# A state-space scan and an ELU layer on one core: the words of the next pair's scan result made on two engines, second-layer steps laid between its last products, and weight words of one group made a step sooner

## The chip, the cores and the metric

The program runs on one core of a Trainium2 chip. The number that counts is the device time of one execution in microseconds (us). The core has a matrix engine (PE, with a separate track PEld for its weight loads), a vector engine (DVE), a scalar engine (ACT), a general engine (POOL), a queue that only issues transfers (SP), and 16 DMA engines. Each engine takes its own instructions in order; between engines, semaphores order the work.

## The reference

The first block is a Mamba-2 scan over 4 batches, 8 heads, 768 positions (head size 32, state size 16), in chunks; the second is a dense layer pair of 256 to 2048 to 256 with an ELU between:

```python
y_intra = np.einsum('bhij,bhjd->bhid', CB * L, xc)                 # inside a chunk
y_inter = np.einsum('bhin,bhnd->bhid', Cc, state) * exp(cum)       # from the state before it
y[:, :, sl] = y_intra + y_inter
...
x = y.transpose(0, 2, 1, 3).reshape(3072, 256)
h = x @ w_in                                                       # first layer, 256 -> 2048
g = np.where(h > 0, h, np.exp(np.minimum(h, 0)) - 1)
out = g @ w_out                                                    # second layer, 2048 -> 256
```

The two weight matrices come as 64-bit floats and are put together as 32-bit floats in the kernel.

## The kernel before, in words

The 3072 tokens are cut into 12 blocks of 256. Blocks 0 to 3 go through the first layer one at a time in plain 32-bit products (`l1`, L666). Blocks 4 to 11 go in pairs (n = 4, 6, 8, 10), 512 tokens at a time, and their first layer is made of "words": both operands are split into a high word and a rest that PE can multiply in its faster `fp32r` form. Three pairs of products per 128 columns (`l1_words`, L770 to L794) write two PSUM tiles, `ps_h` (high words and low words) and `ps_w` (a product of sums, `y_both` with `w_words`). ACT copies `ps_w` to `e` (L787), DVE adds it into `ps_h` (L790), ACT makes the two parts of the ELU in `begin_end` (L796, L797) and DVE ends it in `end_words` (L804), which is called inside the next `l1_words`.

The words of the scan's result come from `words_of_y` (L749) and `both_of_y` (L763): for each of the two halves k of the 256 features, `y1` is y times a constant (L756), `y0` is a difference (L758), and `y_both` a sum (L768). All six are DVE instructions on 128 x 512 elements. The words of `w_in` come from `words_of_w` (L731), once for each of the eight 256-column pieces: an ACT multiplication (L736) and a DVE one (L737).

The second layer of a pair is `second` (L863), a generator. It works by Strassen-Winograd: two halves of seven "quarters", each quarter four `yield`s, 56 steps in all. A step is two 32-bit products of 128 x 128 x 128 (L898), each done by PE in two passes, so four PE records and four weight loads. After a quarter's fourth step its sums are taken out of PSUM by `add` on DVE (L876) or a copy on ACT. Quarters use in turn one of the seven buffers of the pool `ps_a`, which everything else shares, and the single buffer of the pool `ps_o`. The quarter r = 5 of the second half and the quarter r = 0 of the next pair's `second` both use that single buffer.

The order of the work is written out by hand. While pair n is in its first layer (k = 0 to 15), `l2s(count)` lays so many steps of the second layer of pair n-2 behind each `l1_words(n, k)`, and the scan of the next pair m = n+2 is laid in between. At k = 9 come the scan's scores, sums and states; at k = 13 `across` (L594, products of C with the chunk's starting state, PSUM tiles `ps_y`, L613) and then `inside` (L622, products inside the chunk, L632). `inside` adds to the same four PSUM tiles and takes them to `yT` by six ACT instructions (L651). With k = 15 the pair is done; 48 of the 56 steps have been laid by then. Then `words_of_y(m)` and `both_of_y(m)` follow, `end_words()` for k = 15, and the eight steps that are left: the quarters r = 5 and r = 6 of the second half. The next instruction of PE is the first product of `l1_words(m, 0)`, behind its six products come the first steps of the next `second`, quarter r = 0. This passage, from k = 13 of one pair to k = 0 of the next, is called a pair boundary here; there are three (m = 6, 8, 10). For m = 4, `words_of_y(4)` and `both_of_y(4)` are called from the loop over the plain blocks (L1222 and L1224).

In that loop (n = 2, 3, eight steps i each), `scan_ahead(2, i)` (L1139) also makes the words of `w_in`, piece by piece, by the list of L1156; the output of a plain block leaves through one ACT copy (`ob`, L829) from the single `ps_o` buffer.

Of the kernel before, what the change touches and what calls it, by code (L numbers as in the profile page):

```python
# [14 lines left out]
ALU = mybir.AluOpType  # L15
ACT = mybir.ActivationFunctionType
# [5 lines left out]
WORD = 2.0 ** 12  # L22
NEAR = 1.0 + 2.0 ** -13
# [8 lines left out]
def kernel(  # L32
# [27 lines left out]
    nc = tc.nc  # L60
# [21 lines left out]
    def psum(shape, name):  # L82
        return p_a.tile(shape, F32, tag="a", name=name)
# [7 lines left out]
    for k in range(4):  # L91
        (nc.scalar if k % 2 else nc.sync).dma_start(
            out=la0[BH * k:BH * (k + 1)],
# [182 lines left out]
    for v in range(2):  # L276
        nc.gpsimd.affine_select(
            out=low16[Q * v:Q * v + Q], in_=low16[Q * v:Q * v + Q], pattern=[[1, Q]],
# [5 lines left out]
        out=hmask, in_=hmask, pattern=[[-N, NH]], compare_op=ALU.is_ge, fill=0.0,  # L284
        base=0, channel_multiplier=1)
    nc.gpsimd.affine_select(
        out=hmask, in_=hmask, pattern=[[N, NH]], compare_op=ALU.is_ge, fill=0.0,
# [8 lines left out]
        out=minus, in0=ident, scalar1=-1.0, scalar2=None, op0=ALU.mult)  # L296
# [213 lines left out]
    def decay(n, q):  # L510

        decay_of(n, 2 * q)
        decay_of(n, 2 * q + 1)
# [82 lines left out]
    def shift(n, v):  # L596


        return 2 * D * v if n else 0
# [21 lines left out]
    def inside(y, *ns):  # L621


        for t in range(2):
            for at, n in enumerate(ns):
                s = st[n]
                for u in range(2):
                    for v in range(2):
                        toks = slice(Q * v, Q * v + Q)
                        for q in range(4):  # L630
                            h, col = 4 * t + q, (D * q + shift(n, v)) % P
                            nc.tensor.matmul(  # L632
                                out=y[t][v][col:col + D, at, u],
                                lhsT=s["x"][toks, u, D * h:D * (h + 1)],
                                rhs=s["M"][h // 2][toks, u, h % 2], start=False, stop=True,
                                tile_position=(Q * v, col), skip_group_check=True)
            n = ns[0]
            if n // 2 not in yT:
                yT[n // 2] = ffn.tile([P, KC, 2, 2, P], F32, tag="yT", name="yT")
            out = yT[n // 2][:, t, n % 2:n % 2 + len(ns)]  # L640
            for v in range(2):
                k = shift(n, v)
                for at in (0, k) if k else (0,):
                    count, src = P - k, (at + k) % P
                    to, src = out[at:at + count, :, :, Q * v:Q * v + Q], y[t][v][src:src + count]
                    if t and n == 1:
                        nc.vector.tensor_copy(to, src)
                    elif n < 4:
                        nc.scalar.copy(out=to, in_=src)
                    else:  # L650
                        nc.scalar.activation(to, src, ACT.Copy, scale=WORD)  # L651
        for n in ns:
            st.pop(n)
# [96 lines left out]
    def words_of_y(n):  # L750

        y = yT[n // 2].rearrange("p k b u i -> p k (b u i)")
        y1 = conv.tile([P, KC, 2 * BLK], F32R, tag="y1", name="y1", bufs=1)
        y0 = conv.tile([P, KC, 2 * BLK], F32R, tag="y0", name="y0", bufs=1)
        for k in range(KC):
            nc.vector.tensor_scalar(  # L756
                out=y1[:, k], in0=y[:, k], scalar1=NEAR / WORD, scalar2=None, op0=ALU.mult)
            nc.vector.scalar_tensor_tensor(  # L758
                out=y0[:, k], in0=y1[:, k].bitcast(F32), scalar=WORD, in1=y[:, k],
                op0=ALU.mult, op1=ALU.subtract)  # L760
        y_words[n] = y1, y0
# [11 lines left out]
    def l1_words(n, m):  # L773

        cols = slice(m % 2 * P, (m % 2 + 1) * P)
        w, w0 = k_words[m // 2]
        w1, both_w, w0 = w[:, 0, :, cols], w[:, 1, :, cols], w0[:, :, cols]
        y1, y0, both_y = y_words[n]
        high, both = psum([P, 2 * BLK], "ps_h"), psum([P, 2 * BLK], "ps_w")
        passes = [(high, w1, y1), (high, w0, y0), (both, both_w, both_y)]  # L780
        for ps, lhs, rhs in passes if m == 0 else passes[2:] + passes[:2]:
            for k in range(KC):
                nc.tensor.matmul(  # L783
                    out=ps, lhsT=lhs[:, k], rhs=rhs[:, k], start=k == 0 and lhs is not w0,
                    stop=k == KC - 1 and lhs is not w1)
        e = ffn.tile([P, 2 * BLK], F32, tag="e", name="e", bufs=2)
        nc.scalar.copy(out=e, in_=both)  # L787
        if late:
            end_words()
        nc.vector.scalar_tensor_tensor(  # L790
            out=high, in0=high, scalar=1.0 - 1.0 / WORD, in1=e, op0=ALU.mult, op1=ALU.add)
        late.append((n, m, high, e))
# [209 lines left out]
    y = across(0)  # L1002
# [132 lines left out]
    def weigh_two(m, q):  # L1135
        weigh(m, q)
        weigh(m + 1, q)

    def scan_ahead(n, i):  # L1139


        m = 4
        if n == 2:
            if i < 2:
                load_b(m + i)
                load_bc(m + i)
                spread_exp(m + i)
            if i == 2:
                spread_cum(5)
                load_x(m)  # L1150
                load_x(m + 1)
            if i > 1:
                decay(m + i // 6, (i - 2) % 4)
            if i > 2:
                turn_part(m + i // 6, i % 3)
            for p in ((), (), (), (), (0,), (1, 2), (3, 4), (5, 6))[i]:  # L1156
                words_of_w(p)
            if i in (5, 6):
                low_of_w(i - 5)
            return  # L1160
        if i == 0:
            turn_part(5, 2)
            scaled(m, nc.gpsimd)
            scaled(m + 1, nc.gpsimd)
        if i < 2:
            decay(m + 1, i + 2)
        if i == 0:
            words_of_w(7)
        if i == 2:
            turn_part(4, 3)  # L1170
            turn_part(5, 3)
            scores(m, m + 1)
            sums(m, m + 1)
            for q in range(4):
                weigh(m, q)
                weigh(m + 1, q)
            states(m)
            states(m + 1)
        if i in (0, 1):
            load_bc(i + 6)  # L1180
        if i == 2:
            for to in (6, 7):
                load_b(to)
                spread_cum(to)
        if i == 1:
            low_of_w(2)
        if i > 5:
            turn_part(6, i - 6)

    def turn_step(n, k, late):  # L1190
        m = n + 2
        if m == NP or k > 7:
            return
        if m == 6:
            steps = [(6, 2), (7, 0), None, (7, 1), None, (7, 2), (6, 3), (7, 3)]
            if steps[k // 2 * 2 + late]:
                turn_part(*steps[k // 2 * 2 + late])
        else:
            at = k // 2 * 2 + late
            turn_part(*[(m, 0), (m, 1), (m, 2), (m + 1, 0), (m + 1, 1), (m + 1, 2), (m, 3), (m + 1, 3)][at])  # L1200
# [75 lines left out]
    for n in range(4, NP, 2):  # L1276
        m = n + 2 if n + 2 < NP else None
        steps = second(n - 2)

        def l2s(count):  # L1280
            for _ in range(count):
                next(steps)

        for k in range(16):
            l1_words(n, k)
            turn_step(n, k // 2 * 2 + 1, k % 2)
            if n == 4 and k % 2 and k < 8:
                next(left)()
            if n == 4 and k in (1, 3, 5, 8, 10):
                low_of_w({1: 3, 3: 4, 5: 5, 8: 6, 10: 7}[k])  # L1290
            if n == 4 and k == 2:
                sum_t1(2, 7)
            if m:
                stage_scan(n, k)
            begin_end()
            if k == 0 and n > 4:
                store(n - 4, 0)
                store(n - 4, 1)
            if not m:
                l2s(4 if k % 2 else 3)  # L1300
                continue
            l2s((3, 3, 3, 3, 3, 3, 3, 3, 4, 4, 2, 2, 3, 3, 3, 0)[k])
            if k == 9:
                scores(m, m + 1)
                sums(m, m + 1)
                for q in range(4):
                    weigh_two(m, q)
                states(m)
                l2s(3)
            if k == 10:  # L1310
                states(m + 1)
            if k == 13:
                inside(across(m, m + 1), m, m + 1)
        if m:
            words_of_y(m)
            both_of_y(m)
        end_words()
        for _ in steps:
            pass
# [35 lines left out]
```

## Time and profile before

| what | value |
|---|---|
| runs of the kernel before | 354.31 us (353.54 to 355.02, 3 runs) |
| the profiled execution | 354.31 us, of which the span of its instructions is 352.4 us |
| around the span | 1.9 us |
| PE busy | 341.7 us, 97% of the span |
| DVE, ACT, POOL busy | 257.6, 230.1, 199.3 us (73%, 65%, 57%) |
| granted PE clock | full in all 40 slices |
| PE instruction queue q8 | 31 packets, 0.51 MB in all |

How to read it: a busy share is an average over stages, and PE matmuls are pipelined, so a record's duration is longer than what the next record has to wait. What one matmul costs is the distance between the starts of two in a row: 112 ns for a pass of L898, 231 ns for a product of L783, some 7 to 15 ns for a product of L613 or L632. A line such as `[0.33 <-DVE c_sum L876]` gives the idle time of the engine before the instruction and what ended it; "issue" stands where the engine waited for nothing that the profile shows.

### The profile page before, as it was taken

The numbers are of one execution on the slowest core, as the hardware profiler recorded it, in microseconds if no ns is written. First come the engines' busy times: TensorE is split into PE (matmuls) and PEld (weight loads), VectorE is DVE, ScalarE is ACT, GpSimd is POOL, SyncE is SP. The second block draws the span as 40 slices with busy tenths as digits, with TensorE's granted clock in tenths as the row PEclk, the third lists the DMA queues.
The fourth block names the chain that finished last, engine by engine and source line by source line (L and its number), as shares of the span: only waits on it lengthen the run. The fifth ranks groups of instructions, "written<-read, shape, count | busy, mean of one in ns | idle before, by whom it ended". The sixth has DMA issues, their size and how long they took to land.

```text
span 352.4 us, 9890 instructions
## 1 busy us (share of the span) xinstructions
PE 341.7 (97%) x3894; PEld 300.8 (85%) x3894; DVE 257.6 (73%) x532; ACT 230.1 (65%) x527; POOL 199.3 (57%) x309
## 2 busy tenths in 40 slices
PE   8889999999999999999999999999999999999996
PEld 5668888887888889798898988899988899999996
DVE  4898979896999868875878775877775856666232
ACT  4789989799525798566599557599557366555000
POOL 5554554563740299985196764196854173455860
PEclk9999999999999999999999999999999999999999
DMA  8969998561152510160331170230000100000002
GB/s 147 235 201 193 299 187 228 112 103 50 46 87 62 125 47 11 19 149 4 91 74 32 12 155 4 74 63 2 3 1 4 60 1 2 1 2 31 31 1 62
DMA packets 72727, 26.50 MB, mean 75 GB/s; under 512 B 57768, under 2 KB 67560, under 8 KB 72680
## 3 DMA queue, kind: packets, MB, share of 16 engines
q1 hardware_dynamic: 70360, 25.60, 31.1%
q8 instruction: 31, 0.51, 0.7%
q10 hardware_dynamic: 2320, 0.26, 0.5%
q14 instruction: 16, 0.13, 0.1%
HBM read 22.51 MB, written 3.34 MB: 73 GB/s over the span
## 4 chain that ended last, share of the span: by engine, by line
PE 67%; DVE 9%; ACT 9%; POOL 7%; issue 3%; SPq 2%; DMA 2%; POOLq 0%; DVEq 0%; ACTq 0%
PE ps_o L898 26%; PE ps_h L666 12%; PE ps_h L783 11%; PE ps_w L783 6%; PE ps_o L823 6%; DVE ps_h L790 2%; POOL g L839 2%; PE ps_y L632 2%; POOL w L839 2%; DMA w<-in_moe_w_in_dram 2%; POOL L L523 2%; DVE g L804 1%; PE ps_g L538 1%; ACT yT L651 1%; DVE y L758 1%
## 5 line engine op out<-in xcount | busy, mean ns | idle before, releaser
L898 PEld LDWEIGHTS ps_o<-w_out,g 128*128 128x128 f32 x640 | 78.4, 191 | 5.9 <-DVE c_sum L876 2.2
L898 PE MATMUL ps_o<-w_out,g 128*128 128x128 f32 x640 | 80.7, 276 | 1.2 <-DVE c_sum L876 1.1
L804 DVE SCALAR_TENSOR_TENSOR g<-e,ps_h 128x512 f32<-128x512 f32 x64 | 43.9, 686 | 33.3 <-ACT e L797 32.9
L796 ACT ACTIVATE e<-ps_h 128x512 f32<-128x512 f32 x64 | 38.2, 597 | 43.5 <-DVE ps_h L790 43.4
L839 POOL TENSOR_TENSOR g<-g 128x256 f32<-128x256 f32 x32 | 23.3, 730 | 72.8 <-DVE g L804 65.4
L666 PE MATMUL ps_h<-yT,w_in 128*128 128x256 f32 (+1 forms) x272 | 60.4, 371 | 2.0 <-POOL w_in L245 1.9
L666 PEld LDWEIGHTS ps_h<-yT,w_in 128*128 128x128 f32 x272 | 48.4, 190 | 9.6 <-POOL w_in L245 3.1
L790 DVE SCALAR_TENSOR_TENSOR ps_h<-ps_h,e 128x512 f32<-128x512 f32 x64 | 44.6, 697 | 10.4 <-ACT e L787 7.5
L787 ACT COPY e<-ps_w 128x512 f32<-128x512 f32 x64 | 36.8, 575 | 19.3 <-PE ps_w L783 19.3
L783 PE MATMUL ps_w<-y_both,w_words 128*128 128x512 f32 x128 | 45.1, 433 | 0.0
L518 ACT ACTIVATE L<-L,ncum 128x64 f32<-128x64 f32 x160 | 42.5, 337 | 0.2
L797 ACT ACTIVATE e<-e 128x512 f32<-128x512 f32 x64 | 40.4, 632 | 2.0
L783 PE MATMUL ps_h<-y,w_words 128*128 128x512 f32 x128 | 40.5, 397 | 0.0
L783 PE MATMUL ps_h<-y,w 128*128 128x512 f32 x128 | 39.7, 391 | 0.0
L898 PE MATMUL ps_o<-w_sum,g 128*128 128x128 f32 x304 | 38.3, 275 | 0.0
L898 PEld LDWEIGHTS ps_o<-w_sum,g 128*128 128x128 f32 x304 | 37.1, 192 | 1.1
L523 POOL TENSOR_SCALAR_AFFINE_SELECT L<-L 64x512 f32<-64x512 f32 x40 | 29.1, 728 | 10.3 <-ACT L L518 8.2
L823 PE MATMUL ps_o<-w_out,g 128*128 128x256 f32 x128 | 30.7, 382 | 0.7 <-ACT ob L829 0.7
L839 POOL TENSOR_TENSOR g<-t,g 128x256 f32<-128x256 f32 x40 | 28.1, 736 | 5.7 <-PE ps_o L898 5.7
L839 POOL TENSOR_TENSOR t<-g 128x256 f32<-128x256 f32 x40 | 28.8, 752 | 2.4 <-DVE g L852 2.1
L783 PEld LDWEIGHTS ps_h<-y,w 128*128 128x128 f32 x128 | 24.0, 188 | 5.6
L839 POOL TENSOR_TENSOR g<-g,t 128x256 f32<-128x256 f32 x40 | 28.1, 736 | 0.2
(130 smaller groups left out, 531.3 us busy)
## 6 DMA issues: line engine op xcount, KB each, us to landing
L<-flat SPq DMA_DIRECT2D x20, 256.0 KB
w<-in_moe_w_out_dram SPq DMA_DIRECT2D x8, 512.0 KB
w<-in_moe_w_in_dram SPq DMA_DIRECT2D x7, 512.0 KB
xr<-in_x_dram SPq DMA_DIRECT2D x24, 128.0 KB
out_dram<-c_sum SPq DMA_DIRECT2D x9, 256.0 KB
bc<-in_B_dram SPq DMA_DIRECT2D x24, 64.0 KB
bc<-in_C_dram SPq DMA_DIRECT2D x22, 64.0 KB
ec<-flat_exp SPq DMA_DIRECT2D x10, 128.0 KB
```

The lines of the kernel that those rows point to most:

```text
L518: nc.scalar.activation(L[:, h, u], L[:, h, u], ACT.Exp, bias=ncum[:, u, row:row + 1])
L523: nc.gpsimd.affine_select(out=part, in_=part, pattern=[[0, 4], [0, 2], [1, Q]], compare_op=ALU.is_ge, fill=0.0, base=0, channel_multiplier=-1)
L666: nc.tensor.matmul(out=ps[:, j, toks], lhsT=w_in[i][:, k, j * P:(j + 1) * P], rhs=yT[n // 2][:, k, n % 2].rearrange("p u i -> p (u i)")[:, ...
L783: nc.tensor.matmul(out=ps, lhsT=lhs[:, k], rhs=rhs[:, k], start=k == 0 and lhs is not w0, stop=k == KC - 1 and lhs is not w1)
L787: nc.scalar.copy(out=e, in_=both)
L790: nc.vector.scalar_tensor_tensor(out=high, in0=high, scalar=1.0 - 1.0 / WORD, in1=e, op0=ALU.mult, op1=ALU.add)
L796: nc.scalar.activation(e, high, ACT.Relu, scale=-1.0)
L797: nc.scalar.activation(e, e, ACT.Exp, scale=-1.0)
L804: nc.vector.scalar_tensor_tensor(out=g_of[n, m].rearrange("p b i -> p (b i)"), in0=e, scalar=1.0, in1=h, op0=ALU.subtract, op1=ALU.max)
L823: nc.tensor.matmul(out=o_of[n][:, ts], lhsT=g_of[n, j][:, m % 2, ts * P:(ts + 1) * P], rhs=w_out[:, m], start=(m == 0 and ts == 0), stop=( ...
L839: nc.gpsimd.tensor_tensor(out=out, in0=in0, in1=in1, op=ALU.subtract)
L898: nc.tensor.matmul(out=ps[:, ts], lhsT=b[:, ts * P:(ts + 1) * P], rhs=a[:, i], start=(i == chunk[0] and ts == 0), stop=(i == chunk[-1]), s ...
```

## The change

Three edits.

In `words_of_y` the two multiplications that make `y1` are taken out of the loop: the half k = 1 goes to ACT, the half k = 0 stays on DVE, and both stand ahead of the two differences `y0`.

```diff
+        nc.scalar.activation(y1[:, 1], y[:, 1], ACT.Copy, scale=NEAR / WORD)
+        nc.vector.tensor_scalar(
+            out=y1[:, 0], in0=y[:, 0], scalar1=NEAR / WORD, scalar2=None, op0=ALU.mult)
         for k in range(KC):
-            nc.vector.tensor_scalar(
-                out=y1[:, k], in0=y[:, k], scalar1=NEAR / WORD, scalar2=None, op0=ALU.mult)
             nc.vector.scalar_tensor_tensor(
                 out=y0[:, k], in0=y1[:, k].bitcast(F32), scalar=WORD, in1=y[:, k],
                 op0=ALU.mult, op1=ALU.subtract)
```

In the loop over pairs, `words_of_y(m)` moves from behind the loop to k = 15, between `l1_words` and `begin_end`. Four of the eight last steps (the quarter r = 5 with its DVE sum) are laid ahead of `both_of_y(m)` and `end_words()`. At k = 13, one of the three steps stays ahead of `across`, and two go between `across` and `inside`.

```diff
         for k in range(16):
             l1_words(n, k)
+            if m and k == 15:
+                words_of_y(m)
...
-            l2s((3, 3, 3, 3, 3, 3, 3, 3, 4, 4, 2, 2, 3, 3, 3, 0)[k])
+            l2s((3, 3, 3, 3, 3, 3, 3, 3, 4, 4, 2, 2, 3, 1, 3, 0)[k])
...
             if k == 13:
-                inside(across(m, m + 1), m, m + 1)
+                y = across(m, m + 1)
+                l2s(2)
+                inside(y, m, m + 1)
         if m:
-            words_of_y(m)
+            l2s(4)
             both_of_y(m)
         end_words()
```

In `scan_ahead` the pieces of `w_in` whose words are made at i = 3 to 6 shift: piece 0 from i = 4 to i = 3, piece 1 from i = 5 to i = 4, piece 3 from i = 6 to i = 5; pieces 2, 4, 5 and 6 keep their place.

```diff
-            for p in ((), (), (), (), (0,), (1, 2), (3, 4), (5, 6))[i]:
+            for p in ((), (), (), (0,), (1,), (2, 3), (4,), (5, 6))[i]:
                 words_of_w(p)
```

## The prediction

> **What bounds the kernel now.** The page comes first.
>
> ```profile
> PE 341.7 (97%) x3894; PEld 300.8 (85%) x3894; DVE 257.6 (73%) x532; ACT 230.1 (65%) x527; POOL 199.3 (57%) x309
> ...
> q8 instruction: 31, 0.51, 0.7%
> ```
>
> PE is busy 97% of the span and the change takes no product from it, so only PE's waits can be won. The second line is kept for later: PE's instructions come in by 31 transfers of 16 KB, and 3894 + 3894 records over 31 is 251, so about 256 instructions a transfer. Next is the list of waits of PE, of which three rows lie in what the change touches (total us, times, longest).
>
> ```profile
> PE ps_y L632 <- issue: 1.9, 3, 0.7
> PE ps_o L898 <- DVE c_sum L876: 1.1, 3, 0.4
> PE ps_o L823 <- ACT ob L829: 0.7, 1, 0.7
> ```
>
> Two come once at each of the three pair boundaries, the third once at a plain block's end. These idle times count from modelled ends; I price from starts. The timeline of the first boundary (m = 6) shows both:
>
> ```profile
> 160.51 1.17 ACT L651 ACTIVATE yT<-ps_y 128x256 f32<-128x256 f32 x3
> ...
> 161.48 0.69 PE L632 MATMUL ps_y<-M,xr 64*32 64x64 f32 x45 [0.74 <-issue]
> ...
> 162.14 1.18 ACT L651 ACTIVATE yT<-ps_y 128x256 f32<-128x256 f32 x3 [0.46 <-PE ps_y L632]
> ...
> 166.60 0.69 DVE L790 SCALAR_TENSOR_TENSOR ps_h<-ps_h,e 128x512 f32<-128x512 f32 x1
> ...
> 167.20 0.57 DVE L756 TENSOR_SCALAR y<-yT 128x512 fp32r<-128x512 f32 x1
> 167.32 0.60 ACT L796 ACTIVATE e<-ps_h 128x512 f32<-128x512 f32 x1 [0.89 <-DVE ps_h L790]
> 167.80 0.69 DVE L758 SCALAR_TENSOR_TENSOR y<-y,yT 128x512 fp32r<-128x512 f32 x1
> ...
> 168.41 0.42 DVE L756 TENSOR_SCALAR y<-yT 128x512 fp32r<-128x512 f32 x1
> 168.87 0.69 DVE L758 SCALAR_TENSOR_TENSOR y<-y,yT 128x512 fp32r<-128x512 f32 x1
> 169.48 1.29 DVE L768 SCALAR_TENSOR_TENSOR y_both<-y,yT 128x512 fp32r<-128x512 f32 x2
> ...
> 170.80 0.62 PE L783 MATMUL ps_w<-y_both,w_words 128*128 128x512 f32 x2
> 171.28 0.75 DVE L876 TENSOR_TENSOR c_sum<-ps_o,c_sum 128x256 f32<-128x256 f32 x2
> ...
> 171.75 1.61 PE L898 MATMUL ps_o<-w_out,g 128*128 128x128 f32 x12 [0.33 <-DVE c_sum L876]
> ```
>
> PE arrives at 171.75 with the first step of the next `second`, whose PSUM tile is the single `ps_o` buffer. Quarter r = 5 was finished by PE near 168.3, but its sum (the first L876 at 171.28) stands in DVE's queue behind six word instructions and `end_words`.
>
> **The sum ahead of `y_both`, words on two engines.** PE's two last products start at 170.80 and 171.03 and each lasts 0.23 before the next can start, so unhindered r = 0 starts at 171.27 instead of 171.75: 0.48 lost. The same three lines at m = 8 read 224.13 and 225.27 (free at 224.59: 0.68 lost), at m = 10 277.46 and 278.38 (277.92: 0.46). Together 1.62 us.
>
> Does the new order free the buffer in time? DVE's starts in a row (the pace, shorter than the durations) are 0.60 for the first L756, 0.61 for L758 and L768, 0.46 for the second L756, and 0.34 for L876 (165.13 to 165.47 in this timeline). New queue at m = 6: L790 166.60, y1 167.20, y0 167.80, y0 168.41, sum of r = 5 169.02, `y_both` 169.36 and 169.97, `end_words` 170.58, sum of r = 6 171.19. The buffer is free at 169.43 (169.02 + 0.41), 1.8 before PE needs it. One L756 (0.46) leaves DVE and one L876 (0.34) steps ahead, so the last `y_both` ends near 170.65, 0.1 earlier than before, and PE needs it at 171.03. At m = 8 the margin is thinnest: 224.17 against 224.36. PE's next waits of this kind hold: the whole 1.62 is gained unless something else moves.
>
> The ACT half costs nothing here. ACT ends its copy (L787) at 166.44, then idles 0.89 until L790 ends. The same form, an ACT multiplication into `fp32r` of 128 x 512, takes 613 ns (L736): 166.46 to 167.07, before 167.32. The new wait is DVE's second y0 on it, at 168.41, late by more than 1 us. Queued behind it on ACT are only the two ELU parts of k = 15, for which `end_words` waits at 170.58. If the cover went, the cost would be 0.2 to 0.6 a boundary. At m = 4 the ACT half follows six `yT` copies that end at 111.87, so it pushes the next ELU (L679 at 112.15) by about 0.3; DVE has one instruction less there, and the first `y_both` product has 0.77 to spare. Zero.
>
> The row against the rule: L736 takes 613 ns on ACT, L756 421 ns on DVE. The Trainium skill, "ScalarE: Activation LUTs", section "Rules for kernel authors", says to put a multiplication on VectorE and not on ScalarE. By it this half should lose 0.19 us at each of four places, 0.8 in all, if ACT were what PE waits for; the row with 0.89 idle says zero.
>
> **Steps between `across` and `inside`.** What would they fill? The gap at 161.48 falls in the middle of `inside`, before an instruction with no semaphore to wait for. From start to start (160.52 to 161.48, 213.97 to 214.69, 267.24 to 268.06) it takes 0.95, 0.72 and 0.82, 2.5 us in all. I read it as PE waiting for its instructions. First: the three gaps stand 1281 and 1279 PE instructions apart in program order, five blocks of 256. Second: queue q8 has one transfer just before each gap, landing at 160.12, 213.30 and 266.69; PE goes on 1.36, 1.39 and 1.37 later. Third: the next transfer starts 1.12, 1.17 and 1.14 after each gap's end, as if a block's first instruction asks for the block after next. So a transfer is asked for about 1.14 before it starts (157.6, 211.2, 264.3), and PE may run only 256 instructions until it is there, 3.5 to 3.8 us later. `across` and `inside` issue 64 and 128 passes, each with a weight load, at 7 to 15 ns: the block is used up in 2.8 us.
>
> The point that decides: at 157.6, 211.2 and 264.3 PE has already begun the three steps of k = 13 (they start at 157.5, 210.9, 264.2). The moved steps lie inside the window in both orders. The same 256 instructions stand between request and gap, only in another sequence. So two steps (0.9 us) later in the row take 0.9 us away from the front, PE runs dry at the same instruction and the same time, and the gap stays. Bounds from the rows: below, nothing is filled (0); above, 0.90 a boundary fills nearly all of 0.95 and the whole of 0.72 and 0.82. I take 0, nearest to the count of instructions, and keep the other end as a rival.
>
> Row against rule once more: transfers land and PE still waits 1.4 us. The Trainium skill, "Runtime: NRT & Kernel Launch", section "Instruction fetch mechanics", agrees on 16 KiB blocks of 256 instructions but says that prefetch is hidden because dispatch is slower than the fill. By that rule the gap is no fetch, and the steps could fill it: 351.0; by the rows 352.6.
>
> What else moves: `across` starts two steps earlier. Its starting states left POOL at 156.3 at the latest, and it would start near 158.0. The sums of r = 3 end some 0.2 later on DVE, before the ELU end it does next at 160.51. Nothing on SP moves.
>
> **A group of `w_in` words sooner.** PE waits at 83.20 for ACT's `ob` copy: 83.20 instead of 82.38, 0.82 lost. Before the copy ACT runs the two L736 of i = 6; one moves to i = 5, one each from 5 to 4 and 4 to 3. That shortens the queue only where ACT rests between:
>
> ```profile
> 66.00:82.60 16.60, 16.38 (x43) 1.00 0.46 88
> ```
>
> ACT is busy 16.38 of these 16.60 us. The same instructions stand ahead of `ob`, so it ends at the same time, less one rest of 0.09 before L679 at 70.79. Bounds: a loss where the shifted words delay a `w_out` piece (0.52 spare at 74.04, and the 0.82 wait that follows swallows it), a gain up to one L736, 0.52. I take 0.09.
>
> **Sum.** 1.62 + 0 + 0.09 = 1.7 us, from 354.31 (span 352.4 plus 1.9 around it; this execution is also the median of the runs shown) to **352.6**. PE is the limit after each boundary, and the spare time of its other waits there is 0.4 or more, or set by PE itself, so I carry the gain whole.
>
> **Rivals.**
>
> *The gap is filled too.* For: two steps take 0.90 us, about a gap. Against: the count of instructions. Then the chain of `yT` copies sets r = 0: the copies' own wait goes (0.46 at m = 6, none at m = 8 where six run on end, 0.33 at m = 10), the last `y_both` ends at 170.2, 224.2, 276.9, and r = 0 starts 1.26, 0.82 and 1.18 earlier. With 0.09: 354.31 - 3.35 = 351.0.
>
> *The gain is given back.* ACT is busy 20.75 of the 22.5 us after the boundary (171.5 to 194), and the chain of copy, L790, L796, L797 does not start sooner, since it waits for the same last word product. If PE, 0.5 ahead, runs into a PSUM buffer that ACT or DVE has not freed, the gain ends there: 354.2. Against: no such wait there has less than 1 us to spare.
>
> *Slower: `across` meets a buffer that ACT still holds.* Before, its fourth tile takes the buffer that the `ps_w` copy of k = 13 frees; at m = 8 this ends at 212.42, just as PE comes. If, 0.9 earlier, a tile still needs that copy, PE's sequencer stands before the point at which the next block is asked for: later by 0.7 (158.34 for 157.64), 1.2 (212.42 for 211.20) and 0.9 (265.19 for 264.28), 2.8 in all: 354.31 - 1.7 + 2.8 = 355.4. It decides as soon as the buffer comes free later than those requests. Against: in the new order r = 4's step asks for a buffer after the four tiles and not before, so one that is free longer is left for them.
>
> **Numbers.** Forecast 0.52, filled gap 0.22, gain given back 0.16, slower 0.10. A run of this kernel can tell about 0.5% from no change (1.8 us; 352.54 is the border). The forecast lies on it: half of its chance is faster. Faster: 0.26 + 0.22 = 0.48. Slower by over 0.5% needs the slow rival together with the gain given back: 0.05. Same: 0.47. The range reaches from 350.6 (filled gap, 0.4 less for the spread of runs) to 354.6 (gain given back, the same spread), and leaves out the slow rival and tails.
>
> **What would show it.** Right: at k = 0 of each new pair L898 follows L783 after 0.23, with no wait for L876; one ACT multiplication stands between L787 and L796 in ACT's idle time; the "issue" gap in L632 remains with 0.7 to 0.95, on 1280 instructions' distance; L823 still waits near 83 for `ob`. Wrong: the gap is gone or lies elsewhere, or a wait for ACT in `across`, or L783 waiting for `y_both`.

## The result and the profile after

The changed kernel takes 352.48 us (median of 6 runs, 352.12 to 352.69); the kernel before, on the same chip, 355.12 us (6 runs, 353.54 to 355.68). The ratio is 0.9932 with a 95% interval of 0.9911 to 0.9953. The profiled execution takes 352.12 us, its span is 350.3 us. From L755 on, line numbers are one higher than before: L784 is the product of `l1_words`, L899 that of `second`, L877 the sum.

The page's engine row:

```profile
PE 341.5 (98%) x3894; PEld 300.8 (86%) x3894; DVE 256.0 (73%) x528; ACT 231.8 (66%) x531; POOL 199.4 (57%) x309
```

The list of PE's waits:

```profile
PE ps_st L568 <- DVE c_sum L877: 0.9, 1, 0.9
PE ps_y L632 <- issue: 0.8, 1, 0.8
...
PE ps_o L824 <- POOL w_out L245: 0.2, 1, 0.2
```

PE's work is the same (341.5 for 341.7 us); what went is waiting. The row of the single `ps_o` buffer behind the sum (three waits) is gone, as forecast. The "issue" row has one wait left of three, which was not forecast. The 0.7 of the wait for `ob` no longer shows as such; one for `w_out` of 0.2 is new. And one wait outside the boundaries grew, at k = 9 of the pair n = 4 (L568, products of the scan's states, at 146.28 before and 146.86 after). In the kernel before its row is:

```profile
PE ps_st L568 <- DVE c_sum L876: 0.6, 1, 0.6
```

PE stands there 0.82 us from start to start before and 1.13 after. The nine profiled executions below that make the words on two engines all show 1.13 to 1.17, the five that do not 0.80 to 0.82. So the two-engine words cost PE some 0.35 us once, ahead of the first boundary. The DVE instruction `end_words` of k = 8 starts 0.45 us after its ELU part ends in the nine and 0.10 in the five; why was not followed up.

The first boundary (m = 6) in the timeline of the changed kernel, PE's rows from k = 13 on:

```profile
157.75 0.60 PE L899 MATMUL ps_o<-w_sum,t 128*128 128x128 f32 x4
158.29 0.83 PE L613 MATMUL ps_y<-bct,Sx 32*64 32x64 f32 x48
159.05 0.71 PE L899 MATMUL ps_o<-w_sum,t 128*128 128x128 f32 x4
159.60 0.61 PE L899 MATMUL ps_o<-w_sum,g 128*128 128x128 f32 x4
160.14 1.51 PE L632 MATMUL ps_y<-M,xr 64*32 64x64 f32 x128
```

and the rows of ACT, DVE and PE from the last copy to r = 0:

```profile
166.35 0.63 ACT L755 ACTIVATE y<-yT 128x512 fp32r<-128x512 f32 x1
166.62 0.69 DVE L791 SCALAR_TENSOR_TENSOR ps_h<-ps_h,e 128x512 f32<-128x512 f32 x1
167.22 0.57 DVE L756 TENSOR_SCALAR y<-yT 128x512 fp32r<-128x512 f32 x1
167.35 0.60 ACT L797 ACTIVATE e<-ps_h 128x512 f32<-128x512 f32 x1 [0.36 <-DVE ps_h L791]
...
167.82 1.29 DVE L759 SCALAR_TENSOR_TENSOR y<-y,yT 128x512 fp32r<-128x512 f32 x2
...
169.03 0.42 DVE L877 TENSOR_TENSOR c_sum<-ps_o,c_sum 128x256 f32<-128x256 f32 x1
...
169.37 1.28 DVE L769 SCALAR_TENSOR_TENSOR y_both<-y,yT 128x512 fp32r<-128x512 f32 x2
...
170.30 0.91 PE L784 MATMUL ps_w<-y_both,w_words 128*128 128x512 f32 x2
170.57 0.68 DVE L805 SCALAR_TENSOR_TENSOR g<-e,ps_h 128x512 f32<-128x512 f32 x1
171.05 1.50 PE L899 MATMUL ps_o<-w_out,g 128*128 128x128 f32 x12
```

The first block shows the moved steps between L613 and L632, and L632 as one row of 128 passes: no gap. The second shows DVE's new queue, in the order forecast and with its intervals (y1, two y0, sum, `y_both`, end: 167.22, 167.82, 169.03, 169.37, 170.57; forecast 167.20, 167.80, 169.02, 169.36, 170.58). The step at 171.05 waits for no sum. But the row at 170.30 has two products in 0.91 us where two take 0.62 without a wait: its second starts at 170.71, when `y_both` is ready (169.37 + 1.28 = 170.65). PE now comes too early for `y_both`, by 0.18 us here and by 0.37 at m = 8.

At m = 10 the gap is still there:

```profile
264.96 1.04 PE L632 MATMUL ps_y<-M,xr 64*32 64x64 f32 x81
266.79 0.71 PE L632 MATMUL ps_y<-M,xr 64*32 64x64 f32 x47 [0.79 <-issue]
```

From start to start, 265.78 to 266.79, it takes 1.01 us.

The change has three parts, and the experiments below take them one by one. "Words edit" stands for the words on two engines, moved to k = 15, with the four steps ahead of `both_of_y`; "split" for the two steps between `across` and `inside`; the third is the list of `w_in` pieces. "Small products" are products whose results nobody uses, added at the start to shift the program.

Because executions differ by up to 1.1 us long before anything that the change touches (the scan's first scores start between 8.04 and 9.12 us), I compare positions and not clock times: the start of quarter r = 0 (the first L898 or L899 after the word products of k = 0) at each boundary, counted from the last product of the states for m = 6 (L568, at 147.23 in the kernel before, 147.49 after). The table gives how much sooner than in the kernel before (24.52, 78.04, 131.15, and 201.96 us at the last product) each kernel gets there. This count starts behind the longer wait at L568; the last column counts the last product from the last product of `inside` for m = 4 instead (109.97 in the kernel before, 239.22 us to the end), and so has that wait in it.

| kernel | m = 6 | m = 8 | m = 10 | last product | last product, from m = 4 |
|---|---|---|---|---|---|
| forecast | 0.48 | 1.16 | 1.62 | 1.62 | 1.62 |
| rival "gap filled too" | 1.26 | 2.08 | 3.26 | 3.26 | 3.26 |
| changed kernel | 0.96 | 1.79 | 2.05 | 2.35 | 2.40 |
| changed kernel, second execution (`e10_after`) | 1.00 | 1.84 | 1.85 | 2.15 | 1.98 |
| words edit alone (`e2_words`) | 0.54 | 1.19 | 1.90 | 2.20 | 2.05 |
| words edit alone, second execution (`e11_words`) | 0.63 | 1.01 | 1.66 | 1.76 | 1.59 |
| split alone (`e1_split`) | 0.24 | 0.25 | 0.04 | 0.03 | -0.15 |
| weight words only (`e3_w_in`) | 0.19 | 0.09 | 0.26 | 0.46 | 0.59 |
| sum ahead only (`e5_sum_only`) | 0.59 | 0.96 | 1.27 | 1.35 | 1.15 |
| two engines only (`e6_two_only`) | 0.43 | 1.00 | 1.44 | 1.43 | 0.85 |
| before + small products (`e8_before_pad`) | 0.34 | 0.34 | 0.60 | 0.60 | 0.42 |
| words + small products (`e7_words_pad`) | 1.01 | 1.84 | 2.88 | 2.98 | 3.02 |
| change + small products (`e12_after_pad`) | 0.96 | 1.78 | 2.57 | 2.66 | 2.08 |
| change + larger products (`e4_after_pad48`) | 0.96 | 1.80 | 2.78 | 2.88 | 2.87 |
| words reordered + small products (`e9_best`) | 1.33 | 2.50 | 3.76 | 3.76 | 3.78 |

Two rows say how far such numbers can be trusted. `e3_w_in` has the instructions of the kernel before from m = 4 on and still ends 0.46 to 0.59 us sooner, and the two executions of the words edit differ by 0.44. So a difference of less than some 0.6 us in the last two columns is not told from the spread of executions; a gap or a wait that can be read at its place is surer than these sums.

### The profile page after: what moved, and what is told of

It is laid out like the page before. It is cut to its first block, busy times and chain, and to the rows that moved or that the text cites. A ratio compares the mean times of both kernels' runs of the same rounds, so it can differ in the third digit from the quotient of the medians.

```text
span 350.3 us, 9883 instructions
## 1 busy us (share of the span) xinstructions
PE 341.5 (98%) x3894; PEld 300.8 (86%) x3894; DVE 256.0 (73%) x528; ACT 231.8 (66%) x531; POOL 199.4 (57%) x309
## 4 chain that ended last, share of the span: by engine, by line
PE 74%; ACT 9%; DVE 8%; issue 3%; SPq 2%; DMA 2%; POOL 0%; DVEq 0%; POOLq 0%; ACTq 0%
PE ps_o L899 31%; PE ps_h L784 14%; PE ps_h L666 11%; PE ps_w L784 7%; PE ps_o L824 5%; DMA w<-in_moe_w_in_dram 2%; DVE ps_h L791 2%; PE ps_y L632 2%; ACT L L518 1%; PE ps_g L538 1%; ACT yT L651 1%; ACT e L797 1%; PE ps_y L613 1%; PE ps_st L568 1%; ACT e L798 1%
## 5 line engine op out<-in xcount | busy, mean ns | idle before, releaser
L899 PEld LDWEIGHTS ps_o<-w_out,g 128*128 128x128 f32 x640 | 78.6, 191 | 3.9 <-ACT p_sum L911 0.5
L899 PE MATMUL ps_o<-w_out,g 128*128 128x128 f32 x640 | 80.3, 275 | 0.3 <-ACT p_sum L911 0.3
L797 ACT ACTIVATE e<-ps_h 128x512 f32<-128x512 f32 x64 | 38.2, 597 | 41.4 <-DVE ps_h L791 41.4
L784 PE MATMUL ps_w<-y_both,w_words 128*128 128x512 f32 x128 | 45.7, 435 | 0.1
L784 PE MATMUL ps_h<-y,w_words 128*128 128x512 f32 x128 | 40.4, 397 | 0.0
L784 PE MATMUL ps_h<-y,w 128*128 128x512 f32 x128 | 39.6, 390 | 0.0
L899 PE MATMUL ps_o<-w_sum,g 128*128 128x128 f32 x304 | 38.3, 275 | 0.0
L899 PEld LDWEIGHTS ps_o<-w_sum,g 128*128 128x128 f32 x304 | 37.1, 192 | 1.0
L784 PEld LDWEIGHTS ps_h<-y,w 128*128 128x128 f32 x128 | 24.0, 188 | 5.5
L784 PEld LDWEIGHTS ps_h<-y,w_words 128*128 128x128 f32 x128 | 23.7, 188 | 5.3 <-DVE g L805 0.2
```

The costliest lines, as they stand in the source:

```text
L784: nc.tensor.matmul(out=ps, lhsT=lhs[:, k], rhs=rhs[:, k], start=k == 0 and lhs is not w0, stop=k == KC - 1 and lhs is not w1)
L797: nc.scalar.activation(e, high, ACT.Relu, scale=-1.0)
L899: nc.tensor.matmul(out=ps[:, ts], lhsT=b[:, ts * P:(ts + 1) * P], rhs=a[:, i], start=(i == chunk[0] and ts == 0), stop=(i == chunk[-1]), s ...
```

## Experiments

Theory after the result: the words edit gives the 1.6 us; the gaps are waits for instruction blocks, and the split makes them go at two boundaries, but PE then meets the word chain on DVE. Rival: the split itself is worth something, as idle time that the two steps fill.

**One edit at a time.** `e1_split` has only the two steps of k = 13 moved, `e2_words` only the words on two engines, moved to k = 15, and the four steps ahead, `e3_w_in` only the list of pieces.

```diff
e1_split
-            l2s((3, 3, 3, 3, 3, 3, 3, 3, 4, 4, 2, 2, 3, 3, 3, 0)[k])
+            l2s((3, 3, 3, 3, 3, 3, 3, 3, 4, 4, 2, 2, 3, 1, 3, 0)[k])
...
-                inside(across(m, m + 1), m, m + 1)
+                y = across(m, m + 1)
+                l2s(2)
+                inside(y, m, m + 1)
```

> Before with only the k = 13 edit (one step, across, two steps, inside). Theory 'fetch, order neutral' (the recorded prediction): the three gaps in inside stay at 0.7 to 1.0 us, ratio 1.000. Theory 'fetch, asked for earlier' (the block is asked for when PE's sequencer, running ahead of the engine, reaches a point; with the steps gone from in front of across that point is reached up to 1 us earlier as seen from inside): gaps gone at m = 6 and 8 as in the changed kernel, left at m = 10. The first L898 of the next pair still waits for the sum of r = 5, which hangs on the chain of yT copies: that chain gains 0.46 at m = 6 and nothing at m = 8, so 0.4 to 0.6 us in all, ratio 0.998 to 0.999, and the wait for L876 grows by 0.5 to 0.9 at m = 6 and 8. Rival 'PE's time is simply won': all of 1.7 us, ratio 0.995.

Measured: 354.47 us (10 runs) to 354.56 of before, ratio 1.0004 (0.9991 to 1.0017): no difference. The gaps are gone at m = 6 and 8 all the same, and 0.73 stays at m = 10. PE's waits, and the first boundary, show who took the time back:

```profile
PE ps_o L898 <- DVE c_sum L876: 1.2, 3, 0.4
...
PE ps_y L632 <- issue: 0.5, 1, 0.5
```

```profile
169.32 1.29 DVE L768 SCALAR_TENSOR_TENSOR y_both<-y,yT 128x512 fp32r<-128x512 f32 x2
...
170.16 1.01 PE L783 MATMUL ps_w<-y_both,w_words 128*128 128x512 f32 x2
170.53 0.68 DVE L804 SCALAR_TENSOR_TENSOR g<-e,ps_h 128x512 f32<-128x512 f32 x1
171.13 0.75 DVE L876 TENSOR_TENSOR c_sum<-ps_o,c_sum 128x256 f32<-128x256 f32 x2
...
171.60 1.16 PE L898 MATMUL ps_o<-w_out,g 128*128 128x128 f32 x8 [0.43 <-DVE c_sum L876]
```

PE loses 0.28 between the two products on `y_both` (two in 1.01 us), then 0.70 for the sum, where before it lost 0.48. The DVE queue sets r = 0 now; the gap was idle time that this queue would have asked for anyway. The rest goes to two more changes between kinds of products at each boundary (L613 to L898 0.15 us and L898 to L632 0.21, where L613 to L632 took 0.15: 0.2 more).

```diff
e2_words
+        nc.scalar.activation(y1[:, 1], y[:, 1], ACT.Copy, scale=NEAR / WORD)
+        nc.vector.tensor_scalar(
+            out=y1[:, 0], in0=y[:, 0], scalar1=NEAR / WORD, scalar2=None, op0=ALU.mult)
         for k in range(KC):
-            nc.vector.tensor_scalar(
-                out=y1[:, k], in0=y[:, k], scalar1=NEAR / WORD, scalar2=None, op0=ALU.mult)
...
+            if m and k == 15:
+                words_of_y(m)
...
-            words_of_y(m)
+            l2s(4)
             both_of_y(m)
```

> Before with only the y words on two engines, moved to k = 15, and the quarter sum ahead of y_both; k = 13 and the w_in list as before. Prediction's first term: L898 after the last L783 with no wait for L876, 1.62 us less, ratio 0.9954; the three gaps in inside stay at 0.7 to 1.0 us. Rival 'given back': the wait for L876 goes but PE waits elsewhere behind it, ratio 0.999 to 1.000.

Measured: 352.23 us (4 runs), ratio 0.9933 (0.9916 to 0.9950), the whole of the change's gain. Its waits of PE:

```profile
PE ps_y L632 <- issue: 2.0, 3, 0.8
...
PE ps_o L824 <- ACT ob L830: 0.6, 1, 0.6
```

All three gaps stay (0.89, 0.99 and 0.72 from start to start), no wait for the sum and none for `y_both` is left. It is ahead by 0.54, 1.19 and 1.90 us at the three boundaries, where 0.48, 1.16 and 1.62 were forecast.

```diff
e3_w_in
-            for p in ((), (), (), (), (0,), (1, 2), (3, 4), (5, 6))[i]:
+            for p in ((), (), (), (0,), (1,), (2, 3), (4,), (5, 6))[i]:
```

> Before with only the list of w_in words shifted. Prediction: 0.09 us less, ratio 1.000, ob still ends near 82.5 and L823 waits 0.7 to 0.8 us. Rival 'the wait is only moved': the wait at 83 falls to 0.2 and a new one of 0.4 near 74 appears (as the trace of the changed kernel has it), 0.2 us less, ratio 0.9993.

Measured: 354.47 us (10 runs), ratio 0.9992 (0.9978 to 1.0005). From the scores at 59.12 to those at 93.74 it takes 34.62 us, before 34.72: 0.10 gained. The five executions with this list take 34.60 to 34.64 there, the nine without 34.69 to 34.72, so it holds, though the timed runs can't show it. The wait for `ob` (PE goes on at 83.20 before, at 83.19 here) shrinks from 0.82 to 0.21, but a new one stands ahead of 74.54 and takes 0.42 from start to start (the second row counts it from a modelled end). It is for a piece of `w_out`, which I put down to ACT's earlier word:

```profile
72.82 1.46 PE L666 MATMUL ps_h<-yT,w_in 128*128 128x256 f32 x6
74.54 1.99 PE L823 MATMUL ps_o<-w_out,g 128*128 128x256 f32 x8 [0.26 <-POOL w_out L245]
```

ACT has hardly any rest in that stretch in the changed kernel either (16.26 us busy of 16.47), so `ob` cannot end much sooner. The row of that stretch, up to the start of `ob` (length and busy time of ACT with its instructions, then clock, DMA share, GB/s):

```profile
66.42:82.89 16.47, 16.26 (x42) 1.00 0.45 84
```

**Are the gaps instruction blocks?** If they are, moving PE's whole program by some places against the border of the blocks moves or removes them, with no step moved. `e4_after_pad48` is the changed kernel with twelve products of one column (24 passes and 24 weight loads, whose results nobody uses) at the very start.

```diff
e4_after_pad48
     idle_product(3)
+    for _ in range(12):
+        nc.tensor.matmul(
+            out=ps_idle[:, 0, 0:1], lhsT=idle, rhs=idle[:, 0:1], start=True, stop=True)
```

> The changed kernel with twelve one-column products (48 PE instructions) added after the idle products at the start, where PE waits for data. They move every later PE instruction by 48 places against the blocks of 256. Fetch theory: the block border that falls 51 instructions into across at m = 10 falls 3 into it, the gap of 1.0 us at m = 10 goes, none appears at m = 6 and 8; 0.3 to 0.8 us less than the changed kernel, ratio to before 0.991 to 0.992. Rival 'the gap is no fetch': it stays at 1.0 us at m = 10, and the time is that of the changed kernel or up to 0.5 us more.

Measured: 357.05 us (12 runs), ratio 1.0050 (1.0022 to 1.0079): slower, where 0.991 to 0.992 was expected, and yet all three gaps are gone. The twelve runs fall into two groups, five at 354.09 to 354.66 and seven at 357.00 to 358.62 us. The profiled one, 354.09, is of the first, and there the added products are not covered by anything:

```profile
4.25 2.99 PE L267 MATMUL ps_idle<-idle 128*128 128x1 f32 x24
7.10 0.60 PE L481 MATMUL ps_x<-low,ident 128*128 128x256 bf16 x4
```

They cost 2.85 us (4.25 to 7.10, 119 ns a pass), as much as this execution gains by the table. What makes the other seven some 3 us longer no trace shows. This says how the padding must be made, not that the gaps were cheap: the next kernels pad with 14 tiny products of 32 x 32 by one column (28 passes and 28 weight loads, 56 places), ahead of the first `l1`, where PE waits in any case.

```diff
e8_before_pad, and the same lines in e7_words_pad, e9_best and e12_after_pad
     w_sum(0, half[1])
+    for r in range(14):
+        q = slice(32 * (r % 4), 32 * (r % 4) + 32)
+        nc.tensor.matmul(
+            out=ps_idle[q, 0, 0:1], lhsT=idle[q, 0:32], rhs=idle[q, 0:1], start=True, stop=True,
+            tile_position=(q.start, q.start), skip_group_check=True)
     l1(0, 0)
```

> Before with the same 56 places. Fetch theory: the gaps go; the first L898 of the next pair hangs on DVE's queue, which follows the yT copies by 0.46, 0 and 0.33, so about 0.8 us less, ratio 0.998, and the wait for L876 there grows from 0.5 to 0.9 or more. Rival 'PE's time is simply won': 2.5 us less, ratio 0.993. Rival 'no fetch': gaps stay, ratio 1.000.

Measured: 354.40 us (10 runs), ratio 0.9995 (0.9976 to 1.0014). Nothing of the order was changed, and all three gaps are gone. So the place of the instructions in the program makes them, and not the order of the work. (The profiled execution took 355.58 us; 3.4 us of it, from 13.8 us on and so far ahead of the boundaries, had half the granted clock.) The time does not move, because r = 0 still waits for the sum, and now for longer (0.70 at each boundary for 0.48, 0.68, 0.46) and for `y_both` before it (0.28 each):

```profile
PE ps_o L898 <- DVE c_sum L876: 1.3, 3, 0.4
```

This is the same outcome as that of `e1_split`, by another way: without the words edit a filled gap is worth nothing that the timed runs show.

With the words edit and the same lines of padding (`e7_words_pad`):

```diff
e7_words_pad, against e2_words
     w_sum(0, half[1])
+    for r in range(14):
...
     l1(0, 0)
```

> The words edit alone (e2) with fourteen one-column products of 32 x 32 (56 PE instructions) laid where PE waits for w_in before the first l1, so that every later PE instruction stands 56 places further on against the blocks of 256. Fetch theory: no gap of over 0.2 us in inside at any boundary; PE gains 0.7 to 1.0 at each, but y_both (on the chain of the yT copies) follows only by 0.5 at m = 6, 0 at m = 8, 0.3 at m = 10, so 0.8 to 1.6 us less than e2, ratio to before 0.989 to 0.991. Rival 'the gap is a wait of another kind': gaps stay, time as e2.

Measured: 352.08 us (6 runs), ratio 0.9924 (0.9899 to 0.9949), span 349.4. No gap, no wait for the sum, but waits of 0.34, 0.36 and 0.18 for `y_both`. In the table it is 2.98 us ahead, 0.8 to 1.2 more than the two executions without padding; the timed medians cannot tell 0.9924 from 0.9933.

**Which half of the words edit?** `e5_sum_only` only lays the four steps ahead of `both_of_y`; `e6_two_only` makes the words on two engines and moves them to k = 15, but leaves the sum behind `end_words`.

```diff
e5_sum_only
             words_of_y(m)
+            l2s(4)
             both_of_y(m)
```

> Before with only the quarter sum of r = 5 ahead of y_both; all six word instructions stay on DVE behind the loop. The sum takes 0.34 ahead of y_both, so the last y_both ends at 171.1, 224.6 and 277.7 and PE, which would need it at 171.03, 224.36 and 277.69, waits 0.1 to 0.3 there instead of 0.46 to 0.68 for the buffer: 1.1 us less, ratio 0.997. If the ACT half is what carries the gain: ratio 0.999 to 1.000.

Measured: 353.62 us (10 runs), ratio 0.9979 (0.9962 to 0.9996). No wait for the sum worth a row; 0.28 for `y_both` at m = 8 (0.09 and 0.12 at m = 6 and 10). It is ahead by 1.35 at the end, of which 0.5 are gaps that were shorter in this execution (0.64, 0.62 and 0.74).

```diff
e6_two_only
+        nc.scalar.activation(y1[:, 1], y[:, 1], ACT.Copy, scale=NEAR / WORD)
...
+            if m and k == 15:
+                words_of_y(m)
...
-            words_of_y(m)
             both_of_y(m)
```

> Before with only the words on two engines (moved to k = 15); y_both and end_words stay ahead of the sum of r = 5. DVE's queue is 0.46 shorter, so the buffer comes free at 171.2, 224.75 and 277.9 against a need at 171.27, 224.59 and 277.92: 0.46 to 0.52 less at each boundary, 1.4 us in all, ratio 0.996. If the sum's place carries the gain: ratio 0.999 to 1.000.

Measured: 353.82 us (10 runs), ratio 0.9978 (0.9963 to 0.9992). One wait for the sum is left, 0.30 at m = 8. It is ahead by 1.43, or 0.85 by the last column, which has the longer wait at L568 in it. Each half alone thus takes most of the wait for the buffer away, by another route (the sum overtakes the words, or the words leave DVE sooner), and each leaves its remainder at m = 8, where the margin was thinnest; the two together leave none. In the timed runs each half is worth less than the profiles say, 0.8 and 0.6 us, against 2.33 (`e2_words`) and 2.10 (`e11_words`) for both; the intervals are wide (0.1 to 1.4 us for each half), and what the rest consists of is open.

**A version with hardly any of these waits, and the change again.** `e9_best` is the words edit with the padding, and with `both_of_y` ahead of the four steps, so that the sum follows `y_both` on DVE. With it on one chip went the changed kernel, the words edit alone, and the changed kernel with the padding.

```diff
e9_best, against e7_words_pad
-            l2s(4)
             both_of_y(m)
+            l2s(4)
```

> The words edit and the small products that shift the blocks of instructions, as in the run before, with the order behind k = 15 changed: both_of_y first, then the four steps of the quarter r = 5, then end_words. The sum of r = 5 now follows y_both on DVE, so the last y_both ends one sum (0.34 us) sooner, and PE's waits for it (0.34, 0.36 and 0.18 in the run with the words and the small products) are gone: about 0.8 us less than that run, near 351.3 us, ratio to the kernel before near 0.990. Rival: the sum is then too late for the buffer again; PE waits 0.1 to 0.3 us for the sum at each boundary in place of the y_both wait, and the time is the same as there, near 352.1.

Measured: 352.01 us (6 runs, 350.50 to 353.38), ratio 0.9931 (0.9907 to 0.9956), span 349.0 in the profile (351.01 us). DVE's row at m = 6:

```profile
169.19 1.28 DVE L769 SCALAR_TENSOR_TENSOR y_both<-y,yT 128x512 fp32r<-128x512 f32 x2
170.39 0.42 DVE L877 TENSOR_TENSOR c_sum<-ps_o,c_sum 128x256 f32<-128x256 f32 x1
```

and PE's at the same place:

```profile
170.29 0.74 PE L784 MATMUL ps_w<-y_both,w_words 128*128 128x512 f32 x2
170.87 1.60 PE L899 MATMUL ps_o<-w_out,g 128*128 128x128 f32 x12
```

The sum ends at 170.81 and the step starts at 170.87, 0.58 after the first of the two products, where 0.45 is the distance without a wait (at m = 10, 274.62 to 275.07). So 0.13 us is left at m = 6, 0.17 at m = 8 (222.60 to 223.22) and nothing at m = 10: the order is just in time. It gains 1.33, 1.17 and 1.26 us at the three boundaries, 3.76 in all, the most of any profile. In the timed runs that is not seen: 351.3 was expected and 352.01 came, with a spread of 2.9 us, and the interval overlaps those of the changed kernel. So it is the order with the fewest waits here, but not shown to be the faster one.

The changed kernel and `e2_words`, both without any further edit:

> The changed kernel once more, beside the words edit alone on the same chip. Theory: the steps between the two scan parts and the weight words are worth nothing, so both kernels agree within 0.1% (352.2 to 352.6), ratio to the kernel before 0.992 to 0.995. Rival: the split fills the gaps when the buffer wait is gone too, and this kernel is 0.5 to 1.5 us faster than the words edit alone.

> The words edit alone once more, beside the whole change on the same chip: 352.2 to 352.6 and the same as the whole change within 0.1% by the theory; 0.5 to 1.5 us slower than it by the rival. It also shows whether the faster pace of the first-layer products between 275 and 325 us (228 in place of 232 ns) belongs to this kernel: if so it comes again, and if the pace is a matter of the execution it does not.

Measured: the changed kernel 352.81 us (7 runs), ratio 0.9951 (0.9932 to 0.9971); the words edit alone 352.49 us (6 runs), ratio 0.9941 (0.9923 to 0.9960). They can't be told apart, and the rival's 0.5 to 1.5 us for the split is out. The first median stands 0.2 above what I expected (352.2 to 352.6). Between 275 and 325 us the words edit does not show the faster pace of its first execution again (231 in place of 228 ns a product).

```diff
e12_after_pad, against the changed kernel
     w_sum(0, half[1])
+    for r in range(14):
...
     l1(0, 0)
```

> The whole change with the same 14 small products that shift the blocks of instructions. Fetch theory: all three gaps are gone without the help of the moved steps, so the moved steps only add their changes between kinds of products, 0.2 us each at three places: 0.4 to 0.8 us above the words edit with the same small products (352.1), 352.5 to 352.9. Rival: the moved steps are worth something by themselves (a later start of the copies of yT costs nothing, PE is busy meanwhile): equal to or below 352.1.

Measured: 352.36 us (4 runs), ratio 0.9938 (0.9920 to 0.9956), all three gaps gone. In the table it stands 0.32 us behind the words edit with the same padding, which would mean that the moved steps only cost where no gap is there; but 0.32 is within the spread of executions (by the last column it is 0.94), and the timed 352.36 and 352.08 come from two series, so this is not shown. As the profiles stand, it is less than the 0.4 to 0.8 expected: up to m = 8, where PE waits for `y_both` in both kernels (0.34 and 0.36 us there, 0.19 and 0.37 here), they cost 0.06, and at m = 10 another 0.25.

## Why the prediction was right, and where its reasons were not

The forecast of 352.6 us holds (352.48, and 352.81 in the second series), but not by all of the steps it named. That it is so close is in part luck: it counts from 354.31, but the kernel before took 355.12 on the same chip, so the gain was 2.64 us where 1.7 was forecast. In the second series it was 1.78 (354.59 to 352.81).

**The 1.62 us of the `ps_o` buffer: right, step by step.** DVE's queue came as written down, the buffer was free in time, `y_both` at m = 8 was in time in `e2_words` where PE comes as late as I had assumed, and the gain stayed: 1.76 and 2.20 us at the last product in two executions of the words edit alone (1.59 and 2.05 by the last column, the wait at L568 included).

**"Zero" for the ACT half: right where it looked, not everywhere.** At the boundaries L755 fills part of ACT's idle time, which goes from 0.89 to 0.36 us ahead of L797, and nothing behind it is later. At m = 4 DVE's second `y0` waits 0.48 us for it (at 112.85), but PE is not later: from the last product of `inside` to the first word product it takes 5.24 us in both kernels. What the prediction left out is the wait at L568, 0.35 us longer wherever the words are made on two engines. The Trainium skill, "ScalarE: Activation LUTs", section "Rules for kernel authors", puts multiplications on VectorE. The prediction had priced this at 0.8 us, if ACT were what PE waits for. In the traces the ACT instruction is the longer one, 0.63 to 0.42 us, and still `e6_two_only` is faster (0.9978): what decides here is which queue PE waits for.

**"PE runs dry at the same instruction and the same time, and the gap stays": wrong at two of three places.** The reading of the gap as a wait for an instruction block is borne out by `e8_before_pad` and the other padded kernels. What fell is that the request stays where it is while the steps move. In the trace's records of queue q8, the transfer ahead of each gap starts 0.14 before, 0.02 after and 0.17 before the start of `across` in the kernel before; in the changed kernel 0.02 after, 0.18 before and 1.11 after. At m = 6 and 8 it moved forward together with `across`, which starts two steps earlier, while the end of the block, in `inside`, now lies behind those two steps: PE gets there 0.9 us later in relation to the request, and the gap goes. At m = 10 the transfer did not move with `across`, and the gap stays at 1.01 us (1.20 in the second execution, 0.72 in both of the words edit alone). What fixes the moment of the request I have not settled. One lead is an estimate from 256 instructions a block, that is 128 passes with their weight loads: 128 passes before the gap lies 3, 9 and 14 passes inside `across` in the kernel before, and 11, 17 and 25 in the changed kernel, deepest at m = 10. A request made when PE's sequencer, a little ahead of PE, reaches that place would come later there; no run tests it. (The prediction gives `across` 64 passes at every boundary; at m = 6 it has 48.)

**"0" for the split: the size was right, for another reason.** The rival "gap filled too" came true at m = 6 and 8 for the most part (0.96 for 1.26, then 0.83 for 0.82), and is the larger part of what puts the changed kernel ahead of the words edit there (1.79 to 1.19 and 1.01 at m = 8). It is paid back: new waits for `y_both` (0.18 and 0.37), two more changes between kinds of products at each boundary, and a longer gap at m = 10. At the last product 0.15 and 0.39 us are left of it in two pairs of executions, less than the spread, and none in the timed runs. I had named "L783 waiting for `y_both`" and "the gap is gone" as signs of an error; both were there, and the two errors are the two sides of one account.

**0.09 for `w_in`: the size was right (0.10).** The wait that I gave as the lower bound, at a `w_out` piece near 74, did come, 0.42 us, and the later wait swallowed it as described. The sign that L823 still waits near 83 held only in part: 0.21 of 0.82 us is left there, since the wait moved.

**The slower rival did not come:** no wait in `across` for a buffer at any boundary. "The gain given back" did come for the split alone, in `e1_split`, though not at the place named: not behind the boundary, in ACT's copies, but at the boundary itself, in the DVE queue.

## What to carry to other kernels

A wait that PE has early in a chain is worth only as much as the next wait on that chain allows: ask which other queue sets the instruction after it, and take that one away first. Here filling a gap of 0.7 to 1.0 us three times was worth nothing measurable as long as DVE's queue set the next step, and it showed (in the profile, not beyond doubt in the timed runs) once the queue was short. If a wait by "issue" falls in a row of very short instructions, test it by moving the whole program by a few dozen instructions before building an explanation on the order.

## What the runs showed of the hardware

**Instruction blocks can stall PE.** In the kernel before PE runs 131 passes of L613 and L632, each with a weight load, in 1.6 us (158.92 to 160.52) and then stands. Over the 21 gaps of the nine executions that have any, the transfer just ahead of the gap takes 0.88 to 1.38 us, PE goes on 1.22 to 1.53 us after it has landed (1.36 in the changed kernel, 265.43 to 266.79), and the gap takes 0.53 to 1.27 us. With 56 places of padding the transfer starts at 154.38 in `e9_best`, 5 us before `across`, and no gap is left. The Trainium skill, "Runtime: NRT & Kernel Launch", section "Instruction fetch mechanics", has the fetch hidden; here a gap of up to 1.27 us shows (m = 8 in `e11_words`), and whether it costs the program anything depends on what PE meets next (`e8_before_pad`).

**The products of the first layer have two paces.** At full granted clock, a `ps_h` product of `l1_words` follows the one before it after 228 ns in some stretches and after 231 to 232 ns in others, and the pace changes within an execution. Between 275 and 325 us the kernel before shows 231.5 ns, `e2_words` 228.2 and `e11_words`, which is the same kernel, 231.3; with 96 products in that stretch that makes 0.3 us. `e3_w_in` shows 228 there as well, with the instructions of the kernel before. So the pace belongs to the execution and not to the kernel, and is a part of why profiles of one kernel differ by 0.4 us at the last product. Its cause stays open.

**A pass of one column takes as long as one of 128 columns when the weights are 128 x 128:** in `e4_after_pad48`, at the start of the program, 111 to 112 ns from start to start in most of the added passes (119 in the mean, since two of the first take 213), where a pass of L899 with 128 columns takes 112 ns later on. The granted clock was full while they ran (4.25 to 7.10); the 0.995 of that execution comes from 3.4 us at half clock later, from 8.2 on.
